# A graph aggregation by sorting: buckets in two parts of 36 and 23 a row instead of three of 29, 20 and 10

## The chip, the cores and the metric

The kernel runs on one core of one Trainium2 chip. The metric is the device time of one execution in microseconds, the median of several runs. In the profile PE is TensorE (PEld its weight loads), DVE is VectorE, ACT is ScalarE, POOL is GpSimd and SP is the engine that only issues transfers.

## The reference

12,500 nodes with 64 features each and 800,000 edges, drawn at random. For every node the features of the sources of its edges are summed, scaled and multiplied by a small matrix:

```python
N, deg, D = 12500, 64, 64          # E = N * deg edges
nsum = _segment_sum(x[src], dst, N)
h_neigh = nsum * deg_inv[:, None]
return x @ w_self + h_neigh @ w_neigh
```

## The kernel before, in words

The sum over edges is made of matrix products of one-hot matrices. For that the edges are sorted into 7,546 **buckets** (a bucket is one block of 128 source nodes with one block of destination nodes; about 106 edges fall in it). Bucket number `b` is one column of a table `sl` in DRAM and of a table `dlT` in SBUF. The work runs in these stages:

1. **Sort.** `make_keys` packs each edge into one 32-bit key, 6,250 keys in each of the 128 partitions. `sort_runs` (line 229, tiles `a` and `b`) sorts every partition with min and max instructions on VectorE. Its last 30 stages are cut along the row into portions, so that the front of the row is finished first. Each portion is a list of steps, and `after_sort` issues them by hand.
2. **Rows.** The buckets, rounded up to 7,552, are cut into parts, and a part into 128 rows of `KPRS[part]` buckets each. For every row `find_rows` counts on ScalarE where it starts in each of the 128 sorted runs (line 459, an activation with a sum), `gather_runs` then fetches with one indirect DMA of GpSimd for each row (line 474, tile `u`) a piece of `LENS[part][0]` keys of each run, and a small memset of `pad` behind it (`pause`). The sorted runs reach DRAM (`d1`) first, by transfers on SP. So before a row of part 0 is fetched, the sort must have finished up to column `CUT[0]`.
3. **Merge.** `merge_runs` merges the 128 pieces of every row on VectorE in 7 levels: first groups of pieces (`GROUPS`), then the groups. `merge_round` (line 285 the first two instructions of a round, line 297 the rest) does six levels; part 0's last level is `merge_last` (lines 316 and 331), whose lower half (up to `LOWER`) ends first.
4. **Buckets.** Each row is now sorted. `count_below` finds the boundary of each bucket in it (part 0 on ScalarE, line 636; the others on VectorE, line 633), an indirect DMA on GpSimd fetches a window for each (line 655, tile `v`), and `decode_buckets` turns the windows into `sl` and `dlT`. Keys that fell outside a window are the leftovers: a few VectorE instructions pick them (line 782), and later each group of rows fetches them with an indirect DMA (line 916, tile `lx`), and a matmul (line 933) adds them.
5. **The loop** (`nodes`): 950 tiles of 8 buckets. For each 28 buckets (3.5 tiles) SP loads `slb`, VectorE makes two one-hot matrices (line 854 `ohs`, line 859 `ohd`), TensorE gathers source features with `ohs` (line 885, into `ct`), ScalarE copies `ct` to `xg` (line 895; some copies go to VectorE, line 893, once `self.changed` is set), and TensorE sums with `ohd` (line 965, into `acc`).

The loop starts when part 0 is decoded. The other parts are merged and decoded inside it: between tiles `sums_and_merge` issues merge instructions on VectorE, as many nanoseconds of them for each tile as `PACE` says (450 for part 1, 335 for part 2). When all parts are decoded, `self.changed` becomes true and some of the copies move from ScalarE to VectorE.

Every engine executes its instructions in the order of issue; that order is the program's, and no scheduler changes it from the sort's last stages on.

Of the kernel before, what the change touches and what calls it, by code (L numbers as in the profile page):

```python
# [32 lines left out]
KPRS = (29, 20, 10)  # L33
# [3 lines left out]
TURN = -(-BASE[2] // 28) * 28  # L37
SPARE = TURN - BASE[2]
assert 128 * KPRS[2] < BASE[1]
# [6 lines left out]
PONG2 = 64 * LENS[2][0]  # L46
FIRST = 96
FROM_TILE = 50
BEFORE = 19
PACE = (0, 450, 335)  # L50
# [5 lines left out]
PCS = (19, 13, 9)  # L56
PCSN = 14
PIECES = (12, 4)
GRP = (2, 4, 7)
# [9 lines left out]
LOWER = 1770  # L69
CLOSE = 32  # L70
BEHIND = 6
NEARLY = 24
# [270 lines left out]
class Kernel:  # L343
# [136 lines left out]
    def merge_runs(self, part, u, pong):  # L480
# [25 lines left out]
        for n in GROUPS[part]:  # L506
            at = first * lens[0]
            level, rs, nr = 0, lens[0], n
            while nr > 1 + (part == 2):
                yield from round_(level, at, 0 if part == 2 else at, rs, nr, filler)  # L510
                rs, nr, level = 2 * lens[level], nr // 2, level + 1
# [4 lines left out]
            while part < 2 and len(done) > 1 and done[-1][0] == done[-2][0]:  # L516
# [8 lines left out]
        if part == 2:  # L525
            assert par[5] == 0 and par[6] == 1 and GROUPS[2] == (64, 64)
            for i in range(2):
                yield from round_(5, 64 * i * lens[0], 2 * i * lens[5], 2 * lens[4], 2)
            yield from round_(6, 0, 0, 2 * lens[5], 2)
# [160 lines left out]
    def decode_buckets(self, part, v, vp, mps):  # L690
# [31 lines left out]
        def turn(k, n, vk, l16):  # L722
# [4 lines left out]
            if part < 2:  # L727
                nc.scalar.activation(view(self.dlT, BASE[part] + k, [[kpr, 128], [1, n]]), ps, AF.Copy)
            else:
# [3 lines left out]
                for r in range(first):  # L733
                    edge = min(max(SPARE - r * kpr, k), k + n)
                    for a, e, to in ((k, edge, BASE[2]), (edge, k + n, -SPARE)):
# [389 lines left out]
    def after_sort(self, es, mps, aps):  # L1125
        tc = self.tc
        runs, run0, other = ExitStack(), ExitStack(), ExitStack()
# [5 lines left out]
        with tc.manual_schedule():  # L1133
            first, *portions, last = self.portions
# [4 lines left out]
            for i, step in enumerate(portions[0]):  # L1139
# [4 lines left out]
            u1, u0, pong = [stack.enter_context(tc.tile_pool(name=f"l2{i}", bufs=1))  # L1144
                            .tile([128, 128 * LENS[p][0] + more], F32, name="u")
                            for i, (stack, p, more) in enumerate(((runs, 1, 0), (run0, 0, 0), (other, 0, JUNK // 2)))]
            self.junk = pong[:, 128 * LENS[0][0]:].bitcast(BF)
            for i, step in enumerate(portions[1]):
# [16 lines left out]
            self.l1ab.close()  # L1165
            part = 1
            counts = None
            n = 0
            for _ in self.merge_runs(0, u0, pong):
                if rows and not self.hold and next(rows, None) is None:  # L1170
                    if part == 1:
                        gathers = self.gather_runs(1, u1)
                        for _ in range(FIRST):
                            next(gathers)
                        rows = self.find_rows(2, mps)
                        part = 2
                    else:
# [4 lines left out]
                        u2 = dl.tile([128, 128 * LENS[2][0]], F32, name="u2")  # L1182
# [8 lines left out]
            self.sums_and_merge(es, mps, aps, u0, u1, u2, runs, run0, other, counts, gathers)  # L1191
# [9 lines left out]
    def sums_and_merge(self, es, mps, aps, u0, u1, u2, runs, run0, other, counts, gathers):  # L1201
# [42 lines left out]
        for n in self.nodes(fin, aps, mps):  # L1244
# [10 lines left out]
            if chain is None and part + 1 < merging:  # L1255
                part += 1
                assert self.rows[part] is (u1, u2)[part - 1]
                if part == 2:
                    second.close()
# [70 lines left out]
```

## Time and profile before

| | |
|---|---|
| median of three runs | 1993.28 us (1989.81 to 2000.18) |
| profiled execution, its own time | 1997.82 us |
| its span in the profile | 1996.1 us |
| VectorE / ScalarE / TensorE / GpSimd busy | 1860.7 / 1316.4 / 963.1 / 1039.2 us |
| first fetch of a row of part 0 (line 474) | 422.9 us |
| first merge instruction (line 285) | 485.0 us |
| first one-hot (line 854), where the loop starts | 877.8 us |
| last one-hot | 1972.5 us |

A time such as 485.0 us counts from the start of the span. Rows of the timeline give the start, the duration, the engine, the line, what is written and read, and in square brackets the engine's idle time before it and what ended that time.

### The profile page before, as it was taken

To read this page: it belongs to the slowest core of one execution; us is meant where nothing else is said; L and a number is where in the kernel's file an instruction comes from. 1 tells how busy PE (TensorE), PEld (TensorE's weight loads), DVE (VectorE), ACT (ScalarE), POOL (GpSimd) and SP (SyncE) were. 2 spreads that over 40 slices of the span, in tenths; PEclk is the share of its full clock that TensorE was granted. 3 is DMA by queue.
4 is the path that set the end of the run, shared out by engine and by line. 5 is a ranking of instruction groups with operands and counts; after the bars stand their busy time and mean duration, and the time that the engine had idled before them with its cause. 6 is when DMAs were issued, how large, how long until landed. Compare 5 with 4: busy or idle time off the path is not lost.

```text
span 1996.1 us, 55979 instructions
## 1 busy us (share of the span) xinstructions
PE 963.1 (48%) x23311; PEld 853.6 (43%) x23311; DVE 1860.7 (93%) x2319; ACT 1316.4 (66%) x2288; POOL 1039.2 (52%) x1093
## 2 busy tenths in 40 slices
PE   0051000000000000025788888787698999879986
PEld 0041000000000000024677777776587888768875
DVE  8999999998999999998799999999899999988985
ACT  7371006538875004435799888888799999978885
POOL 1000000048888886799898997986232233432331
PEclk9965555555555555568899999988999999999998
DMA  4362000001100001257687888888588888978994
GB/s 147 65 147 46 0 0 18 17 26 39 19 19 18 14 15 44 62 170 186 183 243 235 249 236 246 238 280 247 162 245 260 267 257 255 304 206 265 276 263 111
DMA packets 193619, 303.51 MB, mean 152 GB/s; under 512 B 140921, under 2 KB 152483, under 8 KB 193100
## 3 DMA queue, kind: packets, MB, share of 16 engines
q1 hardware_dynamic: 98124, 273.66, 42.3%
q0 software_dynamic: 86656, 25.95, 9.3%
q8 instruction: 184, 3.01, 0.6%
q10 hardware_dynamic: 8576, 0.24, 0.3%
q14 instruction: 79, 0.65, 0.1%
HBM read 276.66 MB, written 22.65 MB: 150 GB/s over the span
## 4 chain that ended last, share of the span: by engine, by line
DVE 48%; POOL 13%; DMA 13%; issue 8%; PE 7%; ACT 5%; SPq 5%; DVEq 0%; POOLq 0%; ACTq 0%
DMA slb<-sl 12%; DVE u L297 11%; DVE b L229 9%; POOL u L474 8%; DVE a L229 8%; DVE ohs L854 7%; DVE ohd L859 6%; SPq L852 5%; PE ct L885 4%; POOL v L655 3%; PE acc L965 3%; POOL pad L389 2%; ACT xg L895 2%; DVE u L285 2%; DVE u L331 2%
## 5 line engine op out<-in xcount | busy, mean ns | idle before, releaser
L895 ACT ACTIVATE xg<-ct 128x1024 f16<-128x1024 f32 x918 | 862.1, 1068 | 125.6 <-PE ct L885 116.8
L474 POOL DMA_INDIRECT u<-d,ix x384 | 531.7, 1385 | 442.3 <-DVE ix L466 374.0
L885 PE MATMUL ct<-xh,ohs 128*128 128x128 f16 x7546 | 538.2, 225 | 64.0 <-DVE ohs L854 26.1
L297 DVE TENSOR_TENSOR u<-u 128x560 f32<-128x560 f32 (+44 forms) x738 | 498.7, 704 | 27.1 <-ACT u L281 17.6
L885 PEld LDWEIGHTS <-ohs 128*128 128x128 f16 x7546 | 458.9, 101 | 96.3 <-issue 44.8
L965 PE MATMUL acc<-ohd,xg 64*128 64x82 f16 x15092 | 399.2, 202 | 60.2 <-ACT xg L895 39.3
L965 PEld LDWEIGHTS <-xg 64*128 64x128 f16 x15092 | 328.6, 97 | 118.8 <-ACT xg L895 43.2
L859 DVE TENSOR_TENSOR ohd<-iota,dlT 128x2296 f16<-128x2296 bf16 x270 | 362.5, 1342 | 0.2 <-PE acc L965 0.2
L916 POOL DMA_INDIRECT lx<-xt,ls x127 | 202.6, 1595 | 297.6 <-PE acc L933 266.2
L854 DVE TENSOR_SCALAR ohs<-slb,pidx 128x3584 f16<-128x3584 bf16 x270 | 326.5, 1209 | 28.0 <-PE ct L885 16.0
L464 PE MATMUL stp<-idf,st 128*128 128x128 f32 x3 | 1.4, 466 | 480.5 <-DVE st L462 480.5
L229 DVE TENSOR_TENSOR b<-a 128x820 f32<-128x820 f32 (+52 forms) x184 | 214.8, 1215 | 7.0 <-ACT a L231 3.1
L459 ACT ACTIVATE junka<-b,c 128x220 bf16<-128x220 f32 (+46 forms) x384 | 170.5, 444 | 70.5 <-DVE b L229 59.4
L464 PEld LDWEIGHTS stp<-idf,st 128*128 128x128 f32 x3 | 0.5, 182 | 481.3 <-issue 263.2
L229 DVE TENSOR_TENSOR a<-b 128x820 f32<-128x820 f32 (+49 forms) x170 | 198.5, 1211 | 4.7 <-ACT b L231 2.3
L281 ACT ACTIVATE u<-u 128x167 f32<-128x167 f32 (+13 forms) x143 | 55.4, 452 | 176.4 <-DVE u L285 171.2
L1041 POOL DMA_DIRECT2D out<-o x27 | 99.0, 3798 | 58.6 <-ACT o L1035 58.4
L725 PE MATMUL tr<-idb,l 128*128 128x128 bf16 x59 | 8.0, 275 | 224.3 <-ACT l L719 224.3
L231 ACT ACTIVATE a<-b 128x1 f32<-128x1 f32 (+44 forms) x57 | 23.2, 422 | 136.1 <-DVE b L229 133.4
L389 POOL MEMSET pad<- 128x100 f32 x445 | 106.0, 238 | 2.0
L655 POOL DMA_INDIRECT v<-d,ix x59 | 79.0, 1339 | 47.3 <-DVE ix L666 21.6
L725 PEld LDWEIGHTS <-l 128*128 128x128 bf16 x59 | 4.6, 119 | 226.8 <-ACT l L719 226.4
(141 smaller groups left out, 838.7 us busy)
## 6 DMA issues: line engine op xcount, KB each, us to landing
slb<-sl SPq DMA_DIRECT2D x1076, 224.0 KB
u<-d,ix POOLq DMA_INDIRECT x384
xt<-xh SPq DMA_DIRECT2D x1, 3136.0 KB
out<-o POOLq DMA_DIRECT2D x25, 123.0 KB
own<-os SPq DMA_DIRECT2D x12, 256.0 KB
out<-os SPq DMA_DIRECT2D x12, 256.0 KB
rd<-dst SPq DMA_DIRECT2D x4, 521.0 KB
rs<-src SPq DMA_DIRECT2D x4, 521.0 KB
```

The lines of the kernel that those rows point to most:

```text
L229: nc.vector.tensor_tensor(view(dst, lo + sh, [[st, g], [1, l]]), x, y, op=op)
L297: nc.vector.tensor_tensor(to, at(cur, ln + lo, n), at(cur, lo + k, n), op=op)
L389: self.nc.gpsimd.memset(self.pad, 0.0)
L459: nc.scalar.activation(junk[:, :n], w, AF.Sign, bias=self.c1[:, 0, c:c + 1], accum_out=a)
L474: nc.gpsimd.indirect_dma_start(out=u[:nr, p * w:(p + 1) * w], out_offset=None, in_=src, in_offset=bass.IndirectOffsetOnAxis(ap=self.start[ ...
L655: self.nc.gpsimd.indirect_dma_start(out=self.v[:, k].bitcast(F32), out_offset=None, in_=flat(self.d2[part], 128 * PITCH2[part]), in_offset ...
L854: nc.vector.tensor_scalar(s.rearrange("p c s -> p (c s)"), b, self.pidx[:, :1], None, op0=OP.is_equal)
L859: nc.vector.tensor_tensor(d, self.iota[:, None].to_broadcast(wide), ix, op=OP.is_equal)
L885: nc.tensor.matmul(ct[:, i * 128:(i + 1) * 128], cols[i][0], self.xh[:, (b0 + i) % NB].rearrange("p a f -> p (a f)"), start=True, stop=True)
L895: nc.scalar.activation(xg[:, :cnt * 128], ct[:, :cnt * 128], AF.Copy)
L916: nc.gpsimd.indirect_dma_start(out=x, out_offset=None, in_=self.xt, in_offset=bass.IndirectOffsetOnAxis(ap=self.left[p][1][:, c:c + 1].bit ...
L965: nc.tensor.matmul(acc[h][:, db % OCT * HN:(db % OCT + 1) * HN], xg[r, i * 128:(i + 1) * 128], d[r], start=db % OCT == 0 and sb == 0, stop ...
```

## The change

The three parts of 29, 20 and 10 buckets a row become two parts of 36 and 23. The sort's last stages come in three portions instead of four. Part 2 disappears with its 128 row fetches, its merges, its bucket search and its decoding; part 0 and part 1 grow. `PACE` is one number, 400, and `u1` takes the place in memory that the sort leaves, as `u2` did.

The core of the diff (smaller cases for `part == 2` are left out of `merge_runs`, `decode_buckets` and `sums_and_merge`):

```diff
-KPRS = (29, 20, 10)
+KPRS = (36, 23)
-LENS = ((56, 92, 156, 280, 504, 936, 1776, 3424),
-        (44, 72, 120, 208, 368, 676, 1264, 2412),
-        (32, 48, 72, 124, 204, 368, 676, 1264))
-GROUPS = ((32, 32, 32, 32), (64, 32, 32), (64, 64))
+LENS = ((68, 112, 188, 336, 612, 1140, 2176, 4204),
+        (48, 80, 132, 228, 408, 760, 1440, 2752))
+GROUPS = ((32, 32, 32, 32), (64, 32, 32))
+COUNTS = 1
-PACE = (0, 450, 335)
+PACE = 400
-PCS = (19, 13, 9)
-PCSN = 14
+PCS = (23, 15)
+PCSN = 19
-GRP = (2, 4, 7)
+GRP = (2, 3)
-LOWER = 1770
+LOWER = 2200
-NEARLY = 24
+NEARLY = 32
@@ after_sort
-            first, *portions, last = self.portions
+            first, portion, last = self.portions
...
-            for i, step in enumerate(portions[1]):
+            for i, step in enumerate(last):
                 step()
                 while i < BEFORE and next(rows) + 1 < EARLY + (128 - EARLY) * (i + 1) // BEFORE:
                     pass
...
                     for _ in self.gather_runs(0, u0):
                         pass
-            tc.nc.sync.dma_start(self.d1[1], self.runs[:, FROM[1]:CUT[1]])
+            tc.nc.sync.dma_start(self.d1[1], self.runs[:, FROM[1]:])
+            self.l1ab.close()
             rows = self.find_rows(1, mps)
-            for step in last:
-                step()
-                for _ in range(2):
-                    next(rows)
-            tc.nc.sync.dma_start(self.d1[2], self.runs[:, FROM[2]:])
...
             for _ in self.merge_runs(0, u0, pong):
-                if rows and not self.hold and next(rows, None) is None:
-                    if part == 1:
...
+                for _ in range(COUNTS):
+                    if rows and not self.hold and next(rows, None) is None:
...
@@ sums_and_merge
-            if gathers and n % 2 and self.picked < n - 1:
-                if next(gathers, None) is None:
-                    gathers = None
-                else:
-                    gathered.append(n)
-            t += PACE[min(merging, 2)]
+            t += PACE
```

**What SP writes of the sorted runs.** The widths are columns of the sorted row; the first two are part 0, up to `CUT[0]` (3,362 columns before, 4,112 now). Before:

```order
L1137 DMA d_0_60<-b 128x1722
L1143 DMA d_0_60<-b 128x1640
L1158 DMA d_1_61<-b 128x2558
L1164 DMA d_2_62<-b 128x1316
L643 DMA d_0_71<-u 128x1770
L646 DMA d_0_71<-u 128x1654
```

Now:

```order
L1131 DMA d_0_60<-b 128x2104
L1137 DMA d_0_60<-b 128x2008
L1152 DMA d_1_61<-b 128x2760
L637 DMA d_0_68<-u 128x2200
L640 DMA d_0_68<-u 128x2004
```

The third write of before is gone, and part 0's reaches 750 columns further. (The last two rows of each are part 0's merged rows.)

**VectorE, where the sort ends and the merges of part 0 begin.** Before, the end of the narrow last portion (403 columns for each of the two instructions of a stage):

```order
L229 TENSOR_TENSOR b<-a 128x1
L229 TENSOR_TENSOR a<-b 128x133x3 x2
L229 TENSOR_TENSOR b<-a 128x200x2 x2
L229 TENSOR_TENSOR a<-b 128x201x2 x2
L229 TENSOR_TENSOR b<-a 128x403 x2
L229 TENSOR_TENSOR a<-b 128x403 x2
L229 TENSOR_TENSOR b<-a 128x404 x2
L285 TENSOR_TENSOR u<-u 128x16x56 x2
L297 TENSOR_TENSOR u<-u 128x16x24 x2
```

Now, the end of the portion in which the row fetches are issued (1,068 columns):

```order
L228 TENSOR_TENSOR b<-a 128x1
L228 TENSOR_TENSOR a<-b 128x355x3 x2
L228 TENSOR_TENSOR b<-a 128x533x2 x2
L228 TENSOR_TENSOR a<-b 128x534x2 x2
L228 TENSOR_TENSOR b<-a 128x1068 x2
L228 TENSOR_TENSOR a<-b 128x1068 x2
L228 TENSOR_TENSOR b<-a 128x1069 x2
L284 TENSOR_TENSOR u<-u 128x16x68 x2
L296 TENSOR_TENSOR u<-u 128x16x36 x2
```

The portion of 30 stages that stood between the fetches of part 0 and its first merge is gone; the first merge now follows the ten stages that are left of the portion in which the fetches are issued.

**VectorE in the loop, at about the 170th pair of one-hots (tile 595).** Before:

```order
L854 TENSOR_SCALAR ohs<-slb,pidx 128x3584
L859 TENSOR_TENSOR ohd<-iota,dlT 128x2296
L297 TENSOR_TENSOR u<-u_2124 128x2x189
L925 TENSOR_SCALAR ohl<-wide,lp_17466 128x2x82
L297 TENSOR_TENSOR u<-u_2124 128x2x182
L297 TENSOR_TENSOR u_2124<-u 128x2x186
```

Now:

```order
L919 TENSOR_SCALAR ohl<-wide,lp_19115 128x2x82
L887 CAST xg<-ct 128x1024
L848 TENSOR_SCALAR ohs<-slb,pidx 128x3584
L853 TENSOR_TENSOR ohd<-iota,dlT 128x2296
L968 COPY g<-acc_19038 128x6x82
```

The merges of part 2 between the one-hots are gone, and copies of `ct` stand there, which ScalarE made before.

More of the change, by code (lines that the diff above doesn't have):

```diff
@@ L508, in merge_runs @@
             level, rs, nr = 0, lens[0], n
[L509 to L510 removed]
+            while nr > 1:
+                yield from round_(level, at, at, rs, nr, filler)
                 rs, nr, level = 2 * lens[level], nr // 2, level + 1
@@ L1254, in sums_and_merge @@
                         lefts[p][1] = n + wait
[L1255 to L1259, printed above, removed]
-                vp = work.enter_context(tc.tile_pool(name=f"v{part}", bufs=1))
-                chain = self.change(part, vp, mps)
+            if part == 0 and not merge:
+                part = 1
+                assert self.rows[1] is u1
+                vp = work.enter_context(tc.tile_pool(name="v1", bufs=1))
+                chain = self.change(1, vp, mps)
                 last = None
```

82 lines of the change are left out of this document (29 added, 53 removed).

## The prediction

> **What bounds the kernel now.** I read the page's shares of busy time first:
>
> ```profile
> PE 963.1 (48%) x23311; PEld 853.6 (43%) x23311; DVE 1860.7 (93%) x2319; ACT 1316.4 (66%) x2288; POOL 1039.2 (52%) x1093
> ```
>
> VectorE is busy nearly everywhere, but 93% is a mean, so I cut the span at the events of the program and asked for the busy time in each stretch. The columns are the stretch, its length, busy time (and instructions) of PE, PEld, DVE, ACT and POOL, the granted clock, the share of the DMA engines, and GB/s:
>
> ```profile
> 422.80:481.00 58.20, 0.00 (x0) 0.00 (x0) 53.09 (x102) 33.19 (x134) 51.48 (x94) 0.50 0.13 38
> 481.00:485.00 4.00, 0.00 (x0) 0.00 (x0) 0.01 (x1) 1.72 (x6) 3.46 (x8) 0.50 0.56 188
> 485.00:790.00 305.00, 0.95 (x2) 0.36 (x2) 289.15 (x398) 132.80 (x483) 269.60 (x380) 0.50 0.09 19
> 790.00:806.70 16.70, 0.00 (x0) 0.00 (x0) 13.92 (x28) 15.03 (x32) 0.00 (x0) 0.50 0.12 51
> 806.70:877.80 71.10, 4.55 (x29) 2.52 (x29) 67.90 (x119) 24.45 (x48) 64.49 (x83) 0.50 0.27 74
> 877.80:982.90 105.10, 64.33 (x1520) 56.90 (x1520) 84.34 (x134) 61.99 (x71) 95.18 (x91) 0.82 0.71 202
> 982.90:1350.10 367.20, 313.55 (x7778) 278.24 (x7774) 364.81 (x477) 321.37 (x415) 323.85 (x283) 0.95 0.84 247
> 1350.10:1527.90 177.80, 141.45 (x3408) 124.55 (x3410) 166.71 (x254) 150.40 (x201) 69.90 (x47) 0.92 0.76 224
> 1527.90:1972.60 444.70, 395.77 (x10236) 355.14 (x10238) 407.56 (x512) 391.08 (x494) 147.41 (x78) 0.97 0.86 258
> 1797.20:1972.60 175.40, 159.80 (x4279) 145.28 (x4279) 152.10 (x148) 145.43 (x168) 48.45 (x24) 0.98 0.87 257
> 1972.60:1996.00 23.40, 7.29 (x204) 6.36 (x196) 5.53 (x8) 4.53 (x11) 5.34 (x3) 0.75 0.16 13
> ```
>
> Three regimes are to be seen. From the first row fetch (422.8) to the loop (877.8) VectorE sorts, merges and decodes, and almost nothing else counts. In the loop from 982.9 to 1350.1 it is busy 364.8 of 367.2 us: one-hots and merges share it, so each merge instruction delays the tiles. After 1797 there are no merges; VectorE idles 23 of 175 us while TensorE is busy 91% of the time and the DMA engines 87%: the tiles have a floor of their own there, 175.4 us for 49 pairs of one-hots, **3.58 us a pair** of 3.5 tiles.
>
> So a microsecond of VectorE before the loop costs a microsecond; one taken out of the loop is worth a microsecond only down to that floor.
>
> **Prices.** Two lengths of the same instruction give VectorE's slope:
>
> ```profile
> 421.87 2.39 DVE L229 TENSOR_TENSOR a<-b 128x1040 f32<-128x1040 f32 x2
> 476.15 1.07 DVE L229 TENSOR_TENSOR a<-b 128x402 f32<-128x402 f32 x2 [0.26 <-ACT b L231]
> 484.99 2.13 DVE L285 TENSOR_TENSOR u<-u 128x896 f32<-128x896 f32 x2 [4.05 <-POOL pad L389]
> ```
>
> (2.39 - 1.07) / 2 / 638 elements is 1.034 ns an element, and 2.39 / 2 less 1,040 of these leaves 0.12 us an instruction.
>
> The Trainium skill (Vector Engine (DVE) Microarchitecture Reference, 5.2 Measured stream behaviour on trn2) states 1.04 ns a column and about 75 ns an instruction after overlap. The slope agrees; the fixed part here is 0.12 us, and I take the row. With the page's 75 ns the loop's credit below, for 204 instructions, would be 9 us smaller, and the sum 2047 us.
>
> **a. The sort before the fetches.** Part 0 now needs 4,112 sorted columns instead of 3,362 (the writes of `d1` on SP, above). Each of the last 30 stages handles each column once, in a min or a max: 750 x 30 x 1.034 ns = **23.3 us** later. The first fetch moves from 422.9 to 446.2, and no cover exists: VectorE is the only worker here.
>
> **b. The cover of the fetches.** The first merge needs 32 fetches of GpSimd:
>
> ```profile
> 422.89 1.13 POOL L474 DMA_INDIRECT u<-d,ix  x1 [373.98 <-DVE ix L466]
> 434.26 1.83 POOL L474 DMA_INDIRECT u<-d,ix  x1 [0.16 <-issue]
> 480.84 0.95 POOL L474 DMA_INDIRECT u<-d,ix  x1 [0.15 <-issue]
> ...
> 629.07 1.21 POOL L474 DMA_INDIRECT u<-d,ix  x1 [0.16 <-issue]
> ```
>
> From the first (422.89) past the 32nd (480.84) to the merge (484.99) takes 62.1 us. Before, 58 us of sorting covered it, and VectorE waited 4.05 us. Now only ten stages of 2 x 1,068 elements are left, 10 x 2 x 1.22 = 24.5 us: the sort ends at about 470, the fetches at 446.2 + 62.1 = 508.3, and **VectorE waits 38 us instead of 4**. In time this adds nothing to a, since both sides come to the same 508.3; what is lost is 36 us of useful work (the old third portion) that once lay in that wait. Nothing in VectorE's order can fill it. The fetches' own price is bounded: at 0.95 us each (beside an idle VectorE) with the gaps and the two memsets 1.7 us, 32 make 54 us, 4 fewer than the 58 here; at 1.83 us, as beside long sort instructions, 2.43 us or 78 us. Before, about ten ran at the slow price and the rest faster; now again ten meet long instructions and the rest an idle engine, so I keep 62.1, range 58 to 82.
>
> The Trainium skill says (SBUF — State Buffer, Who interferes with whom) that a VectorE instruction with two SBUF inputs contends with a GpSimd instruction that reads SBUF; 1.83 us against 0.95 us agrees with it. Were all 32 fetches held back so, the first merge would come 20 us later; but VectorE is idle for most of them.
>
> **c. Part 0's merges.** By `merge_plan` and `LENS`, part 0 grows from 233,018 elements in 376 instructions to 290,260 in 388: 57,242 x 1.034 ns + 12 x 0.12 = **60.6 us**, all on the path (VectorE is busy 289 of 305 us there). GpSimd's 128 + 96 row fetches run beside them as before: part 1's start when part 0's are issued (629.07, quoted above, 206 us after the first), now at about 446 + 206 = 652 us, in time for its merges after 870.
>
> **d. Search, windows, decoding.**
>
> ```profile
> 804.62 0.85 ACT L636 ACTIVATE u<-u,c 128x667 bf16<-128x667 f32 x1
> 806.72 0.95 POOL L655 DMA_INDIRECT v<-d,ix  x1 [21.64 <-DVE ix L666]
> 855.07 1.44 POOL L655 DMA_INDIRECT v<-d,ix  x1 [0.16 <-issue]
> ```
>
> ScalarE's counts behind the last merge are 15 in 14.7 us now; 18 of up to 738 elements make 18.7, **4 us** more. The 29 window fetches take 48.35 / 28 = 1.73 us each; 7 more are **12.1 us**. VectorE is as full as GpSimd here, with 6 us of extra merges of part 1 and 3 of decoding, which fit inside.
>
> The loop starts at 877.8 + 23.3 + 60.6 + 4 + 12.1 = **977.8**, 100 us later.
>
> **e. The loop.** What VectorE no longer does in it, by counting its instructions behind the first one-hot: merges fall from 426 instructions and 207,216 elements to 222 and 127,194, 204 x 0.12 + 80,022 x 1.034 ns = 107 us. Bucket counts rise from 13,607 elements in 30 (line 633, 20.4 us) to 28,376 in 23, some 34 us, so 14 more. Copies rise from 32 to 67:
>
> ```profile
> L895 ACT ACTIVATE xg<-ct 128x1024 f16<-128x1024 f32 x918 | 862.1, 1068 | 125.6 <-PE ct L885 116.8
> L893 DVE CAST xg<-ct 128x1024 f16<-128x1024 f32 x32 | 39.0, 1220 | 24.4 <-PE ct L885 23.7 <-issue 0.5 <-ACT o L1035 0.3
> L297 DVE TENSOR_TENSOR u<-u 128x560 f32<-128x560 f32 (+44 forms) x738 | 498.7, 704 | 27.1 <-ACT u L281 17.6
> L633 DVE TENSOR_SCALAR_CACHE_REDUCE junk<-u,c 128x103 bf16<-128x103 f32 (+29 forms) x30 | 20.4, 680 | 0.1
> ```
>
> 35 x 1.22 = 43 us, given away by ScalarE, only where VectorE has room. By stretch, cut at the same pairs of one-hots as above:
>
> - 20 pairs from 877.8: before 105.1 us with 20.8 of idle. One wait is most of it:
>
> ```profile
> 956.84 1.24 DVE L854 TENSOR_SCALAR ohs<-slb,pidx 128x3584 f16<-128x3584 bf16 x1 [12.91 <-PE ct L885]
> 951.62 0.95 POOL L916 DMA_INDIRECT lx<-xt,ls  x1 [0.16 <-issue]
> ```
>
>   TensorE waited for the first leftovers (`lx`), which stood behind 14 row fetches of part 2 in GpSimd's queue. Those are gone; `lx` follows part 1's last fetch directly. 105.1 - 12.9 - 3 of fewer merges = 89.2.
> - 90 pairs (982.9 to 1350.1): 315 tiles. `PACE` falls from 450 to 400 ns for about 275 of them (13.8 us) and rises from 335 for 40 (2.6); part 1's search (some 9 us of line 633) moves out. 367.2 - 20 = 347.2, above the floor of 90 x 3.58 = 322.
> - 40 pairs (1350.1 to 1527.9): part 2's merges leave (40 us), part 1's rest, search and decoding come (12 of merges, 34 of counts): 177.8 - 3 = 175, against a floor of 143.
> - 119 pairs (1527.9 to 1972.6): no merge and no part is left, so the floor: 119 x 3.58 = 426 instead of 444.7. VectorE's removed work is worth 19 us here, not the 49 of its merges.
>
> Sum 1037.4 instead of 1094.8, **57 us back**. With 23.4 behind the last one-hot as before the span is 977.8 + 1037.4 + 23.4 = **2038.6** against 1996.1, 2.1% more. The profiled execution took 1997.82, 1.7 above its span and 0.23% above the median of 1993.28; on that scale 2040.3 is **2036 us**.
>
> **The rivals.**
>
> *The loop gives all of it back* (same or faster). Its floor could be lower than 3.58: in that stretch TensorE is busy 159.8 of 175.4 us. If the tiles ran at that, the last 119 pairs take 388 us, and with the third stretch at VectorE's bare sum (165) the span is 1990.6, -0.3%. It decides once the loop is under 995 us. For it speaks that GpSimd has little left to do; against it that ScalarE and VectorE, relieved, did not reach it in the 49 pairs seen. Chance 0.13.
>
> *VectorE's total decides* (faster). The sort and the merges lose 246 instructions and 13,396 elements, 43 us; at 93% busy the span would follow, to 1953. Against it: 34 us of new idle before the merges, and the floor. The Trainium skill's rule (VectorE: DVE Perf Modes, Rules for kernel authors) to minimize the operation count speaks for this case; the trace bears it out only where VectorE is full. Chance 0.05.
>
> *Part 1's search stalls the tiles* (slower still). Its windows now reach 2,278 elements, 2.4 us in a piece before a one-hot, 23 times; if TensorE loses 1.1 us at each, 25 us more: 2064 in the span, about 2061. Before, the two chains cost 11.1 us of VectorE idle in 1350 to 1528. Chance 0.17.
>
> My own sum has 0.65, with 2010 to 2060. To leave out no more than 2 in 10, the range is 2000 to 2062: most of the first rival is outside it. 0.5% is about what a measurement here can tell: slower by more 0.82, within 0.08, faster 0.10.
>
> **What would show it.** Right: first fetch near 446, a VectorE wait of some 35 us ended by GpSimd before the first merge, part 0's merges about 365 us long, first one-hot near 978, no 13 us wait for `lx`, and about 3.6 us a pair from tile 525 on. Wrong: a first one-hot before 950, or fewer than 3.4 us a pair in the last stretch.

## The result, and the profile after

The changed kernel takes **2057.42 us** (median of four runs, 2051.18 to 2061.83) against 1991.68 for the kernel before in the same comparison: ratio 1.0319, 95% interval 1.0278 to 1.0361 (times are medians, ratios here and below are of means). The forecast was 2036 with 2000 to 2062: the sign and the range held, the size was 21 us short. The profiled execution took 2055.87 us, its span is 2054.1. Its busy times, to set beside the line of before:

```profile
PE 954.5 (46%) x23292; PEld 852.0 (41%) x23292; DVE 1866.9 (91%) x2040; ACT 1223.4 (60%) x1965; POOL 808.0 (39%) x825
```

VectorE does the same amount of work, 1866.9 us against 1860.7, in 58 us more. So nearly all of the loss is idle time of VectorE, and three windows show where it lies: up to the first row fetch, from there to the first one-hot, and the loop. First before, then after (columns as in the prediction: length, then busy time of PE, PEld, DVE, ACT and POOL):

```profile
0.00:422.80 422.80, 35.26 (x152) 29.53 (x152) 407.63 (x300) 179.80 (x398) 8.48 (x32) 0.64 0.20 52
422.80:877.80 455.00, 5.50 (x31) 2.88 (x31) 424.07 (x643) 207.19 (x703) 389.03 (x563) 0.50 0.13 33
877.80:1972.60 1094.80, 915.09 (x22934) 814.83 (x22936) 1023.42 (x1372) 924.85 (x1177) 636.34 (x496) 0.94 0.82 243
```

```profile
0.00:446.10 446.10, 37.93 (x152) 31.88 (x152) 429.79 (x318) 180.84 (x411) 7.30 (x29) 1.00 0.20 50
446.10:992.40 546.30, 5.93 (x37) 3.29 (x37) 473.54 (x595) 159.09 (x456) 411.58 (x581) 1.00 0.13 31
992.40:2031.40 1039.00, 902.46 (x22883) 809.70 (x22884) 957.69 (x1123) 877.84 (x1088) 383.80 (x213) 0.95 0.84 252
```

Length less the third busy time is VectorE's idle time: 15.2, 30.9 and 71.4 us before, 16.3, 72.8 and 81.3 after. The work moved from the loop (65.7 us less there) to the front (71.6 us more), as the change says; on the way 42 us of idle time appeared in the middle window and 10 in the loop.

The stages of the changed kernel in the cut of the prediction (part 0's merges, counts behind them, windows and decoding, then 20, 90, 40 and 119 pairs of one-hots, and the tail):

```profile
505.80:885.50 379.70, 0.48 (x1) 0.18 (x1) 352.81 (x409) 111.36 (x355) 280.43 (x382) 1.00 0.09 18
885.50:905.90 20.40, 0.00 (x0) 0.00 (x0) 18.29 (x30) 18.63 (x38) 0.04 (x1) 1.00 0.12 50
905.90:992.40 86.50, 5.45 (x36) 3.10 (x36) 78.69 (x136) 27.60 (x56) 78.47 (x101) 1.00 0.28 77
992.40:1075.50 83.10, 67.26 (x1566) 60.15 (x1566) 81.43 (x123) 61.67 (x68) 55.13 (x47) 0.90 0.84 248
1075.50:1419.80 344.30, 304.24 (x7743) 271.14 (x7738) 340.98 (x410) 315.32 (x398) 113.30 (x49) 0.98 0.84 250
1419.80:1606.50 186.70, 145.06 (x3408) 127.21 (x3405) 166.86 (x233) 150.09 (x215) 81.35 (x55) 0.90 0.77 234
1606.50:2031.40 424.90, 385.90 (x10177) 351.20 (x10177) 368.42 (x362) 350.75 (x410) 134.02 (x62) 0.97 0.87 263
2031.40:2054.00 22.60, 8.17 (x224) 7.16 (x221) 5.84 (x8) 5.67 (x11) 5.33 (x3) 0.77 0.16 14
```

And the two rows at the seam between sort and merges, the first fetch and the first merge instruction, with the idle time of each engine before it:

```profile
446.15 1.15 POOL L473 DMA_INDIRECT u<-d,ix  x1 [397.33 <-DVE ix L465]
505.81 1.29 DVE L284 TENSOR_TENSOR u<-u 128x1088 f32<-128x1088 f32 x1 [35.49 <-POOL pad L388]
```

| step | forecast, us | measured, us |
|---|---|---|
| first fetch | 446.2 | 446.15 |
| first merge (VectorE's wait before it) | 508.3 (38) | 505.8 (35.5) |
| part 0's merges | 365.6 | **379.7** |
| counts behind them | 20.7 | 20.4 |
| windows and decoding | 83.2 | 86.5 |
| first one-hot | 977.8 | 992.4 |
| loop by 20 / 90 / 40 / 119 pairs | 89.2 / 347.2 / 175 / 426 | 83.1 / 344.3 / 186.7 / 424.9 |
| loop | 1037.4 | 1039.0 |
| tail | 23.4 | 22.7 |

One term is off by much: part 0's merges, by 14 us of the 15.5 that the span missed. The rest of the 21 us is how far a profiled execution lies from the median: the one of before, on which the sum was scaled, was 4.5 us over its median of then, and this one is 1.6 under.

Where the 14 us are, the groups of instructions of that stretch tell (busy time, mean of one, idle time before them and what ended it). After, VectorE's two lines and ScalarE's copies; then the same of before, in its stretch of 305.0 us:

```profile
L296 DVE TENSOR_TENSOR u<-u 128x752 f32<-128x752 f32 (+29 forms) x324 | 263.3, 845 | 24.5 <-ACT u L280 18.0
L280 ACT ACTIVATE u<-u 128x512 f32<-128x512 f32 (+12 forms) x62 | 29.9, 520 | 253.1 <-DVE u L284 252.5
```

```profile
L297 DVE TENSOR_TENSOR u<-u 128x704 f32<-128x704 f32 (+28 forms) x312 | 214.5, 728 | 12.5 <-ACT u L281 7.5
L281 ACT ACTIVATE u<-u 128x512 f32<-128x512 f32 (+10 forms) x62 | 23.0, 432 | 126.0 <-DVE u L285 126.0
```

VectorE's busy time grew by 63.7 us (289.15 to 352.81), 3 more than forecast. Its idle time grew by 11 (15.9 to 26.9), and the forecast had no growth there: 10.5 of that are waits for ScalarE's copies in `merge_round` (line 280: keys that a round leaves where they are still have to be copied to the other buffer).

A round shows how. After its first two instructions (line 284) ScalarE copies, and VectorE goes on with the pair of the first distance. VectorE in one group of 32 pieces, rounds of 8, 4 and 2 pairs of runs, and ScalarE's copies in the last of these:

```profile
524.02 0.58 DVE L296 TENSOR_TENSOR u<-u 128x168 f32<-128x168 f32 x2 [0.88 <-ACT u L280]
524.96 11.08 DVE L296 TENSOR_TENSOR u<-u 128x640 f32<-128x640 f32 x12 [0.36 <-ACT u L280]
539.07 11.43 DVE L296 TENSOR_TENSOR u<-u 128x388 f32<-128x388 f32 x14 [1.20 <-ACT u L280]
550.53 1.63 DVE L284 TENSOR_TENSOR u<-u 128x672 f32<-128x672 f32 x2
553.88 3.36 DVE L296 TENSOR_TENSOR u<-u 128x82 f32<-128x82 f32 x6 [1.72 <-ACT u L280]
```

```profile
552.19 1.66 ACT L280 ACTIVATE u<-u 128x590 f32<-128x590 f32 x3 [4.35 <-DVE u L284]
```

The last round is the clearest: line 284 ends at 552.16, the three copies run from 552.19 to 553.85, and VectorE's first pair starts at 553.88. It doesn't run beside the copies; it waits for them to their end. The program's order with the semaphores that each instruction waits for says the same. These are the first pairs of those rounds, now and, in the round of 4 pairs of runs, before:

```
352 L296 TENSOR_TENSOR u<-u 128x8x21 [waits Activation_49]
368 L296 TENSOR_TENSOR u<-u 128x4x97 [waits DVE_49,Activation_49]
384 L296 TENSOR_TENSOR u<-u 128x2x41 [waits DVE_49,Activation_49]
...
427 L297 TENSOR_TENSOR u<-u 128x4x65 [waits DVE_49]
```

`Activation_49` is ScalarE's semaphore. In part 0's 22 rounds in `merge_round` the first pair carries this wait 12 times now and 4 before; VectorE's idle time ahead of these first pairs adds up to 15.6 us now and 3.1 before. Where it doesn't, at most a later pair waits, and the first covers the copies for as long as it lasts. The same round of before:

```profile
509.55 1.53 DVE L285 TENSOR_TENSOR u<-u 128x624 f32<-128x624 f32 x2
511.11 0.77 DVE L297 TENSOR_TENSOR u<-u 128x260 f32<-128x260 f32 x2
512.14 8.65 DVE L297 TENSOR_TENSOR u<-u 128x496 f32<-128x496 f32 x12 [0.26 <-ACT u L281]
```

The round ahead of it has a first pair of 8 elements (0.26 us for both instructions), and its second pair waits 1.38 us.

The new sizes did two things at once: they made copies longer (590 elements for each pair of runs in the last round shown, where the plan's first distance was 64 and is 128, instead of 182), and they put the wait ahead of the first pair in eight more rounds. By the plan, the ranges that pair and copies write do not overlap; why the wait is set in some rounds and not in others was not found. No run moves the wait alone, so how the 10.5 us divide between the two is not shown. The kernel has a switch, `late`, that issues the copies behind the first instruction of the first pair; it is off in part 0, and no run turned it on there.

### The profile page after: what moved, and what is told of

The parts are those of the page before. It is cut to its first block, busy times and chain, and to the rows that moved or that the text cites. A ratio compares the mean times of both kernels' runs of the same rounds, so it can differ in the third digit from the quotient of the medians.

```text
span 2054.1 us, 55077 instructions
## 1 busy us (share of the span) xinstructions
PE 954.5 (46%) x23292; PEld 852.0 (41%) x23292; DVE 1866.9 (91%) x2040; ACT 1223.4 (60%) x1965; POOL 808.0 (39%) x825
## 4 chain that ended last, share of the span: by engine, by line
DVE 22%; DMA 13%; PE 12%; issue 7%; POOL 6%; ACT 5%; SPq 3%; DVEq 0%; ACTq 0%; POOLq 0%
DMA slb<-sl 11%; DVE u L296 7%; PE ct L879 6%; DVE ohs L848 5%; PE acc L959 4%; DVE ohd L853 4%; ACT xg L889 3%; POOL u L473 3%; SPq L846 3%; POOL v L649 2%; DVE u L330 2%; DVE u L284 1%; POOL pad L388 1%; ACT u L630 1%; DMA lk<-lt 1%
## 5 line engine op out<-in xcount | busy, mean ns | idle before, releaser
L889 ACT ACTIVATE xg<-ct 128x1024 f16<-128x1024 f32 x883 | 831.4, 1057 | 132.2 <-PE ct L879 109.2
L473 POOL DMA_INDIRECT u<-d,ix x256 | 332.1, 1297 | 440.5 <-DVE ix L465 397.3
L296 DVE TENSOR_TENSOR u<-u 128x570 f32<-128x570 f32 (+43 forms) x578 | 464.4, 831 | 33.0 <-ACT u L280 23.9
L959 PE MATMUL acc<-ohd,xg 64*128 64x82 f16 x15092 | 389.3, 202 | 52.2 <-ACT xg L889 22.6
L910 POOL DMA_INDIRECT lx<-xt,ls x118 | 211.4, 1792 | 510.3 <-PE acc L927 495.8
L228 DVE TENSOR_TENSOR b<-a 128x1008 f32<-128x1008 f32 (+44 forms) x154 | 211.3, 1421 | 4.2 <-ACT a L230 0.3
L280 ACT ACTIVATE u<-u 128x512 f32<-128x512 f32 (+14 forms) x110 | 50.0, 507 | 272.0 <-DVE u L284 271.5
L228 DVE TENSOR_TENSOR a<-b 128x1008 f32<-128x1008 f32 (+38 forms) x140 | 194.8, 1436 | 4.0 <-ACT b L230 2.0
L458 ACT ACTIVATE junka<-b,c 128x220 bf16<-128x220 f32 (+44 forms) x256 | 115.3, 450 | 47.1 <-DVE b L228 39.8
L230 ACT ACTIVATE a<-b 128x1 f32<-128x1 f32 (+44 forms) x57 | 23.4, 425 | 165.6 <-DVE b L228 162.8
L887 DVE CAST xg<-ct 128x1024 f16<-128x1024 f32 (+1 forms) x67 | 80.9, 1209 | 45.2 <-PE ct L879 35.9
```

The source lines that it names most:

```text
L228: nc.vector.tensor_tensor(view(dst, lo + sh, [[st, g], [1, l]]), x, y, op=op)
L296: nc.vector.tensor_tensor(to, at(cur, ln + lo, n), at(cur, lo + k, n), op=op)
L458: nc.scalar.activation(junk[:, :n], w, AF.Sign, bias=self.c1[:, 0, c:c + 1], accum_out=a)
L473: nc.gpsimd.indirect_dma_start(out=u[:nr, p * w:(p + 1) * w], out_offset=None, in_=src, in_offset=bass.IndirectOffsetOnAxis(ap=self.start[ ...
L889: nc.scalar.activation(xg[:, :cnt * 128], ct[:, :cnt * 128], AF.Copy)
L910: nc.gpsimd.indirect_dma_start(out=x, out_offset=None, in_=self.xt, in_offset=bass.IndirectOffsetOnAxis(ap=self.left[p][1][:, c:c + 1].bit ...
```

## The experiments

Experiments 1 to 4, 5 to 8 and 9 to 11 ran in three groups, each beside runs of the kernel before. Spans and events are of profiled executions; up to the first one-hot those of the same kernel repeat within 1.5 us, the loop's last stretch within 5.

**1. The sort in four portions again.** The cut at column 5,442 comes back, and the last columns are sorted while the fetches run.

```diff
-    for last in [SPLIT] + CUT[:-1]:
+    for last in [SPLIT] + CUT[:-1] + [5442]:
...
-            first, portion, last = self.portions
+            first, portion, last, tail = self.portions
...
+            for step in tail:
+                step()
```

> The changed kernel with the sort's last stages cut in four portions again: the portion in which the row fetches of part 0 are issued ends at column 5442 (1330 columns instead of 2138), and the last 958 columns are sorted behind the fetches, as before the change. Mine (the lost cover costs nothing by itself, the later fetch does): the 20 stages ahead of the first fetch are 17 us shorter for VectorE, but ScalarE needs some 40 us there for 64 row counts of 0.63 us, so the first fetch comes about 8 us earlier (438 instead of 446), the first merge at about 498, VectorE's wait before it shrinks from 35 to about 20 us, and the time falls by about 8 us, to some 2049 against the changed kernel's 2057. Rival (the lost cover itself costs the 31 us by which the wait grew): about 2026.

Measured: 2033.16 us, ratio to before 1.0167 (1.0125 to 1.021). The first fetch comes at 438.8, and the wait shrinks from 35.5 us to 7.6:

```profile
492.94 1.29 DVE L284 TENSOR_TENSOR u<-u 128x1088 f32<-128x1088 f32 x1 [7.60 <-POOL pad L388]
```

The first one-hot comes 12.8 us earlier (979.6). So filling 28 of the 35.5 us of idle time was not worth 28: it moves VectorE's work from before the fetches to beside them, and the merges still can't start before 32 fetches are done. The chain gains 7.3 us by the earlier first fetch and 5.3 because the fetches themselves take 51.4 us instead of 56.7 up to the 32nd. The loop took 1028.5, 10 us less than in the profile above and 6 less than in the control below, nearly all of it in the last stretch (416.3), for which no mechanism was found. In time the gain was 24 us, between my 8 and the rival's 31; the part of it ahead of the loop has the cause above.

**2. Smaller first groups**: two groups of 16 in place of the first 32, so that the merges wait for 16 fetches.

```diff
-GROUPS = ((32, 32, 32, 32), (64, 32, 32))
+GROUPS = ((16, 16, 32, 32, 32), (64, 32, 32))
```

> The changed kernel with part 0's first group of 32 runs cut in two groups of 16, so that the first merge needs 16 fetches instead of 32. Mine (VectorE stands still there for want of fetches, and each microsecond of it is on the path): the first merge at about 483 instead of 506, some 28 us of merging run while the other 16 rows are fetched; against it stand about 46 more merge instructions (5 us) and more waits for ScalarE's copies (3 us). About 15 us less than the changed kernel: 2042. Rival (only VectorE's sum of work counts): 5 us more, 2062.

Measured: 2051.40 us, 1.0252 (1.0201 to 1.0302).

```profile
481.14 1.48 DVE L284 TENSOR_TENSOR u<-u 128x544 f32<-128x544 f32 x2 [10.80 <-POOL pad L388]
```

The first merge comes 24.7 us earlier, the first one-hot only 10.5 (981.9): the extra group has rounds and instructions of its own (64 more instructions, where 46 were expected, and 25.5 us of waits for copies instead of 18.0), and their price takes back more than half.

**3. Shorter distances** in the plan of the rounds, to give the copies and the first pairs other sizes.

```diff
-SIGMA = 6.0
+SIGMA = 5.5
```

> The changed kernel with a bound of 5.5 sigma instead of 6 on how far a key can stand from its place when two runs are merged. With it part 0's fourth and sixth merge levels need no distance of 128 and 256, as in the kernel before, where the shorter runs did not need them, and ScalarE's copies of the untouched keys between two merge instructions are shorter (26182 to 22028 elements over part 0). Mine (the 14 us by which part 0's merges came out longer than forecast are this: VectorE's waits for ScalarE's copies, 18.0 instead of 7.5 us, and the extra steps): about 5 us of instructions and 9 us of waits less before the loop, 2043. Rival (the excess is VectorE slowed by GpSimd's fetches, or waits for the fetches): the 5 us of instructions alone, 2052.

Measured: 2048.40 us, 1.0249 (1.0203 to 1.0294). Part 0's merges take 373.8 us instead of 379.7, and the first one-hot comes at 985.9.

```profile
L296 DVE TENSOR_TENSOR u<-u 128x864 f32<-128x864 f32 (+29 forms) x312 | 259.3, 862 | 22.5 <-ACT u L280 16.3
```

The first distances are those of the kernel before again, but the waits only fell from 18.0 to 16.3 us; the other 4.4 are instructions. So the length of the distance, my first reading of the 14 us, is not what makes VectorE wait. That led to the rows on the semaphores above: in this kernel, too, the first pair carries the wait in three of the five rounds of a group.

**4. Fewer merges for each tile.**

```diff
-PACE = 400
+PACE = 350
```

> The changed kernel with 350 instead of 400 ns of merge instructions a tile in the loop, so that part 1's merges end some 50 tiles later. Mine (the loop has a floor of about 3.58 us a pair of one-hots, and VectorE's work counts only where a pair exceeds it): pairs with merges fall from 3.83 to about 3.66 us, and fewer pairs are left at the floor: about 14 us less, 2043. Rival (VectorE's sum decides the loop, so where its work stands makes no difference): 2057.

Measured: 2040.99 us, 1.0203 (1.0149 to 1.0258). The loop's stretches:

```profile
992.30:1072.30 80.00, 64.12 (x1519) 57.06 (x1520) 78.31 (x119) 60.30 (x67) 64.08 (x46) 0.91 0.90 254
1072.30:1403.30 331.00, 301.63 (x7727) 268.75 (x7726) 328.97 (x399) 311.46 (x393) 117.03 (x49) 0.98 0.88 260
1403.30:1565.50 162.20, 137.97 (x3424) 122.69 (x3424) 157.78 (x161) 141.26 (x183) 72.20 (x43) 0.93 0.84 256
1565.50:2017.00 451.50, 397.90 (x10257) 358.14 (x10252) 387.23 (x438) 372.58 (x459) 142.16 (x76) 0.96 0.85 252
```

1024.7 instead of 1039.0. The merges move 27 us into the last stretch, where VectorE had room, and the three stretches ahead of it, where VectorE is the limit, give 41 back. This is the split that the forecast of the loop was made by.

**5. The changed kernel once more**, as a control for the next three.

> The changed kernel once more, unchanged, beside the next three kernels on one chip, so that each of them can be compared with it event by event. Expected: first one-hot within 2 us of 992, span 2050 to 2060. If the loop's last 119 pairs differ by more than 5 us from the 425 of the first profile, differences of that size in the last stretch of other kernels mean nothing.

Measured: 2055.67 us, 1.0294 (1.0247 to 1.034); first one-hot 991.8, span 2049.1, the stretches 83.1, 344.4, 186.2 and 420.8. Up to the last stretch all repeats within half a microsecond; the last is 4 us shorter.

**6. Part 0's size alone**: three parts and four portions as before, but part 0 at 36 buckets a row.

```diff
-KPRS = (29, 20, 10)
+KPRS = (36, 13, 10)
-LENS = ((56, 92, 156, 280, 504, 936, 1776, 3424),
-        (44, 72, 120, 208, 368, 676, 1264, 2412),
+LENS = ((68, 112, 188, 336, 612, 1140, 2176, 4204),
+        (36, 60, 92, 156, 264, 472, 868, 1640),
```

> The kernel before with its first part at the new size and the rest still in two: 36, 13 and 10 buckets a row, four portions of the sort, three parts. Theory (the size of part 0 costs, wherever the rest is cut): first fetch at 446, part 0's merges about 380 us, first one-hot between 975 and 1000, 100 to 120 us later than before; in the loop the merges of parts 1 and 2 shrink by 50 us of VectorE only, so the loop takes about 1055 and the span about 2065. Rival (the two parts and the three portions cost, not part 0's size): the first one-hot stays near 900 and the span under 2010.

Measured: 2065.82 us, 1.0337 (1.0291 to 1.0383); first one-hot 979.1, span 2063.3; the loop's stretches 88.6, 387.6, 144.8 and 440.3. Part 0's merges and what lies between them and the loop:

```profile
492.40:872.90 380.50, 0.95 (x2) 0.37 (x2) 353.26 (x410) 142.63 (x491) 283.08 (x382) 0.50 0.08 17
872.90:979.10 106.20, 5.48 (x36) 3.11 (x36) 91.10 (x189) 46.43 (x97) 76.66 (x115) 0.50 0.25 71
```

Part 0's merges take 380.5 us, as in the changed kernel (379.7). The size of part 0 alone costs 101 us ahead of the loop, of which the loop gives 33 back. Cutting the rest into one part instead of two, and the sort into three portions instead of four, is then worth 9 us to the good (2063.3 to 2054.1): 13.3 lost before the loop, 22.3 won in it.

**7. ScalarE's copies twice**, in part 0's merges; the second writes the same values again.

```diff
     def both():
-        for a, e in alone:
-            nc.scalar.activation(at(src, a, e - a), at(oth, a, e - a), AF.Copy)
+        for _ in range(2 if ln in LENS[0] else 1):
+            for a, e in alone:
+                nc.scalar.activation(at(src, a, e - a), at(oth, a, e - a), AF.Copy)
```

> The changed kernel, with each of ScalarE's copies of untouched keys in the merges of part 0 issued twice (the second rewrites the same values). Those 62 copies take 29.9 us of ScalarE. Theory (VectorE stands still for these copies at nearly every level: its first pair of a level waits for their end where an order row shows an Activation wait on it): part 0's merges get 18 to 30 us longer, 398 to 410 instead of 380, and the first one-hot comes at 1010 to 1022. Rival (the copies are hidden behind VectorE's own pairs, and the idle time seen is a fixed signal delay): under 5 us longer.

Measured: 2075.95 us, 1.0379 (1.0336 to 1.0422); first one-hot 1015.7, 23.8 us later than the control. VectorE's line and the copies in that stretch:

```profile
L297 DVE TENSOR_TENSOR u<-u 128x752 f32<-128x752 f32 (+29 forms) x324 | 263.0, 844 | 47.7 <-ACT u L281 41.7
L281 ACT ACTIVATE u<-u 128x512 f32<-128x512 f32 (+12 forms) x124 | 58.8, 519 | 247.1 <-DVE u L285 245.7
```

28.9 us more of copies make 23.7 us more of VectorE's waits, at the same busy time. So VectorE pays four fifths of each microsecond that these copies take: the rival, a fixed delay of signals, is out.

**8. Groups of 32, 32 and 64**: 82 instructions and five rounds fewer for the same elements.

```diff
-GROUPS = ((32, 32, 32, 32), (64, 32, 32))
+GROUPS = ((32, 32, 64), (64, 32, 32))
```

> The changed kernel with part 0's 128 pieces merged in groups of 32, 32 and 64 instead of four of 32: the same 290,260 elements in 82 instructions fewer and five rounds fewer. Theory (each instruction costs 0.12 us beside its elements, and each round has its own wait for ScalarE's copies): part 0's merges 9.8 us shorter by the instructions and 2 to 5 by the waits, so 365 to 368 instead of 380, first one-hot at 977 to 981. Rival (the group of 64 waits for its last row fetch): the fetches end near 655 and the group starts near 650, so a wait of about 5 us there, and 3 to 7 us of gain in all.

Measured: 2050.38 us, 1.027 (1.0221 to 1.0318); first one-hot 989.6, only 2.2 us earlier than the control. The group of 64 found its last pieces missing, for longer than the 5 us that the rival gave it:

```profile
662.00 2.43 DVE L284 TENSOR_TENSOR u<-u 128x2176 f32<-128x2176 f32 x1 [12.48 <-DMA u<-d,ix]
L296 DVE TENSOR_TENSOR u<-u 128x768 f32<-128x768 f32 (+40 forms) x252 | 254.8, 1041 | 20.1 <-ACT u L280 14.8
```

Beside that wait the parts came as priced. Line 296 is busy 254.8 us instead of 263.3, and line 284 42.6 instead of 43.8 (34 and 44 instructions): 9.7 us for 82 instructions, 0.118 each. The waits for copies fell by 3.2. The Trainium skill (Vector Engine (DVE) Microarchitecture Reference, 5.2) gives about 75 ns an instruction; an estimate by it would be 6.2 us. The 9.7 us measured decide for the prediction's 0.12.

**9. No copies of `ct` on VectorE**: ScalarE makes all of them.

```diff
-            pend.append(gather(b0, cnt, self.changed))
+            pend.append(gather(b0, cnt, False))
```

> The changed kernel without the 67 copies of `ct` that VectorE takes over once all parts are decoded: ScalarE makes all 950. Theory (the last 119 pairs run at a floor that TensorE and the DMA engines set, and the copies only fill VectorE's room): the stretch stays at 421 to 430 us and the span within 6 us of 2052. Rival (ScalarE is just as near its limit, and the floor of 3.5 us a pair exists only because VectorE takes these copies): 67 copies of 0.94 us make ScalarE up to 63 us longer, of which it has some 40 free, so the stretch takes 440 to 455.

Measured: 2056.72 us; ratio 1.0176 (1.0107 to 1.0245), in a group of runs in which the kernel before itself took 2022.89, some 25 us more than in the others, so that this ratio and the next two aren't set beside earlier ones. First one-hot 992.8, and the last 119 pairs:

```profile
1608.00:2029.00 421.00, 386.96 (x10168) 347.54 (x10168) 313.93 (x315) 394.73 (x469) 119.61 (x63) 0.98 0.89 268
```

421.0 us, as in the control (420.8), with ScalarE busy 394.7 instead of 350.8 and VectorE 313.9 instead of 368.3. Neither sets the floor of the last stretch. What is left near its limit in that row is TensorE (387 of 421) and the DMA engines (0.89); which of the two it is, no run tells.

**10. What helped, together**: the four portions, the pace of 350, and one pause behind each of the first 32 fetches (`CLOSE = 0` instead of 32).

> What helped the changed kernel, together: the sort in four portions again, 350 ns of merges a tile instead of 400, and one pause instead of two behind each of the first 32 row fetches. Theory (the parts add up: they act at different places): first merge near 486 and first one-hot at 972 to 976, the loop 14 us shorter than that of the four portions alone (1028.5), so a span of 2008 to 2014, still slower than before. Rival (the last stretch takes the 14 us back): a span near 2025.

Measured: 2037.22 us (median of ten), 1.0064 (1.0031 to 1.0098) to before in that group; beside the 1992 to 1999 us of before in the other groups it would be about 1.02. The profiled execution took 2045.76 us, the longest of the ten, so some 8 us of the loop below are likely that execution's alone. First merge 491.2: the second pause was worth 1.7 us, not 7. The 32 fetches were issued in 47.4 us instead of 51.4, but the merge then started 4.2 us after the end of the last of them instead of 1.8. First one-hot 978.4, and the loop 1043.0, where 1014 were expected:

```profile
978.50:1066.80 88.30, 69.69 (x1531) 61.20 (x1532) 78.36 (x119) 61.61 (x68) 54.21 (x45) 0.88 0.80 233
1562.40:2021.50 459.10, 398.19 (x10228) 357.49 (x10229) 386.35 (x438) 371.73 (x458) 140.20 (x76) 0.96 0.83 248
```

The rival had the direction: the first stretch is 8 us longer and the last 8 us longer than with the pace alone, with the same busy time of VectorE and a DMA share of 0.80 and 0.83 instead of 0.90 and 0.85. In the first stretch most of it is not this kernel's doing. The kernel of experiment 9 has there the instructions of the changed kernel, which took 83.1 us for it in both profiles, and in this group of runs it took 89.0:

```profile
992.80:1081.80 89.00, 70.53 (x1566) 60.92 (x1566) 81.50 (x122) 62.13 (x68) 42.44 (x44) 0.86 0.79 232
```

What made that group slower there, and whether it also made the last stretch longer, stays open.

**11. Two parts of 33 and 26**, with four portions. Part 1 has to be ready sooner, which takes a pace of 500.

```diff
-KPRS = (36, 23)
+KPRS = (33, 26)
...
-PACE = 400
+PACE = 500
```

> The changed kernel with two parts of 33 and 26 a row instead of 36 and 23, four portions of the sort, and 500 ns of merges a tile (fewer and part 1 would not be ready when the tiles reach it). Theory (three buckets a row fewer in part 0 save about 42 us before the loop, and the loop pays about two thirds of it back as merges of part 1): first merge near 486, first one-hot at 934 to 942, the loop 1050 to 1062, the span 2008 to 2024. Rival (the loop pays nothing, since its floor is the tiles'): a loop of 1030 and a span of 1990. Third (VectorE's total decides, the span stays): 2028 to 2034.

Measured: 2042.89 us, 1.0108 (1.0041 to 1.0176) in the same group; first one-hot 929.8, loop 1086.8, span 2039.0.

```profile
929.80:1020.70 90.90, 70.20 (x1535) 61.03 (x1536) 87.10 (x127) 62.59 (x71) 59.93 (x49) 0.89 0.78 228
1020.70:1394.70 374.00, 314.32 (x7719) 279.57 (x7716) 370.07 (x428) 316.04 (x395) 124.27 (x54) 0.93 0.77 229
1394.70:1596.50 201.80, 149.04 (x3417) 129.20 (x3410) 175.29 (x241) 153.18 (x222) 82.27 (x60) 0.88 0.72 219
```

My forecast of the loop failed. 50 us saved before it (against the first experiment) came back as 58 in it, nearly all in the three stretches up to the 150th pair, and the span moved by 8. About 6 of the 58 are the first stretch's, which that group of runs made longer for experiment 9 too. That is nearest to the third case, that VectorE's total decides: its busy time is 12 us longer than in the first experiment (1886.2 and 1874.4). My reading is that two thirds would be paid back only if the merges that move into the loop found room there; here they all stand ahead of the 110th pair, where VectorE is nearly full (370 of 374 us in the second stretch), and none in the last stretch, where it is not.

**12. The kernel before, against itself.**

> The kernel before once more, unchanged, timed against itself and profiled, since it was 1993, 1999, 1999 and 2023 us beside the groups of runs so far while the changed kernel stayed near 2056. Expected: a ratio of 1 with an interval that holds 1 (0.995 to 1.005). The stages up to the first one-hot repeat within 2 us (first merge 485, first one-hot 878); theory: what differs from look to look lies in the loop's stretches (105.1, 367.2, 177.8, 444.7 in the first profile), above all in the last. Rival: it lies before the loop.

Measured: 1995.86 against 1996.7 us, ratio 0.9987 (0.9966 to 1.0008). First merge 485.0, first one-hot 879.1, the loop's stretches 104.4, 366.7, 175.2 and 442.0: the profile that the forecast was read from repeats within 3 us in each. The 2022.89 of the group above was not seen again and is not explained.

No version of the changed kernel was faster than the kernel before.

## Why the prediction was right, and where it was not

- **The sort before the fetches** (a) and **the cover of the fetches** (b) came as worked out: first fetch 446.15 for 446.2, wait 35.5 for 38, first merge 505.8 for 508.3. That the wait adds nothing to the later first fetch is shown by the first experiment: filling 28 us of it moved the first one-hot by 12.8, and that by the fetches. It also shows that "nothing in VectorE's order can fill it" was wrong: the end of the sort can, and with less of the sort ahead of them the fetches start 7.3 us earlier.
- **Part 0's merges** (c) is the step that was mis-sized: 60.6 us priced, 74.7 measured. Elements and instructions were within 3 us. The sentence "VectorE is busy 289 of 305 us there" was taken for "nothing waits", and the 16 us of idle time were left as they were, though 7.5 of them were waits for ScalarE's copies that grow with the part, and whose cover depends on which instruction carries the wait. Doubling the copies showed the price of that term (23.7 us for 28.9).
- **Search, windows, decoding** (d): counts 20.4 for 20.7; windows and decoding 86.5 for 83.2, since the 36 fetches took 1.80 us each up to the last (905.9 to 969.0 for 35 of them) instead of 1.73.
- **The loop** (e): 1039.0 and 1034.5 for 1037.4. The floor of the last stretch held: 3.57 and 3.54 us a pair for 3.58, and experiment 9 shows that ScalarE's and VectorE's shares are not behind it. The 13 us wait for the first `lx` is gone. The 40 pairs around part 1's search are 11.7 us longer than forecast, against 9 us won in the two stretches ahead, so that the total came this close partly by luck. Bucket counts there are busy 34.4 us, as forecast. Of the 11.7 us, 3 are busy time that the forecast took off and that did not go, and 8.7 are idle time of VectorE (19.8 us there, 11.1 before). The 3 came from terms that do not add up as written: 40 us that leave and 12 and 34 that come make 6 more, and only with line 285's 8.6 us of before 3 less. Nor is the idle time the third rival's (the search stalls the tiles): the counts run from 1440 to 1515, and VectorE's waits from 1534 to 1562, behind them, are 13.8 us, while part 1 is decoded. The longest is a chain. ScalarE waits 6.02 us for a transfer of the decoding (`sl<-l`) before it goes on to copy `ct`, TensorE waits 7.78 us for that copy, and VectorE 4.98 us for TensorE; in the control the same chain waits 3.76, 5.52 and 3.54 us. VectorE's waits ahead of its one-hots in the stretch, then the three of the chain:

```profile
L848 DVE TENSOR_SCALAR ohs<-slb,pidx 128x3584 f16<-128x3584 bf16 x40 | 49.7, 1243 | 13.9 <-PE ct L879 7.3 <-DMA slb<-sl 6.7
1538.51 0.72 ACT L708 ACTIVATE l<-w,edge 128x512 bf16<-128x512 int32 x1 [6.02 <-DMA sl<-l]
1541.47 0.73 PE L959 MATMUL acc<-ohd,xg 64*128 64x82 f16 x16 [7.78 <-ACT xg L889]
1546.22 1.15 DVE L848 TENSOR_SCALAR ohs<-slb,pidx 128x3584 f16<-128x3584 bf16 x1 [4.98 <-PE ct L879]
```

- **The rivals.** That the loop gives all back needed a loop under 995 us; none of eleven profiles of the changed kernel and its variants was under 1024. That VectorE's total decides was wrong for this change (busy time up 6 us, span up 58). Its 43 us counted sort and merges alone; with the copies (43 us) and bucket counts (14 us) that (e) adds to VectorE, the prediction's own prices give 14 us more, not 43 less. Still, the last but one experiment shows that between two ways of cutting in two it comes close.
- **The sum by 75 ns an instruction** (2047 us) takes the whole 9 us off the loop's credit, though (e) adds the loop up by stretches and cuts the last one at its floor; by (e)'s own working less than 9 us of it would reach the sum.

## What to carry to other kernels

When work moves from a stage where it shares an engine with others to one where it runs alone, compare the engine's idle time by stage, not its total: here VectorE's work was the same to 6 us, and 52 of the 58 us lost were new idle time. Price the short waits inside a stretch that looks full: read what ends them, and ask whether that work grows with the change and which instruction carries the wait. An idle gap in front of a chain of transfers is worth only what the chain gets shorter, not its length.

## What the runs showed of the hardware that I had not expected

GpSimd's row fetch takes longer the longer the VectorE instructions beside it are; that VectorE is busy costs it little by itself. The fetches beside sort instructions of 1.2 us, beside an idle VectorE, and (first experiment) beside sort instructions of 0.25 to 0.5 us, with a row of VectorE from the first and the third:

```profile
L473 POOL DMA_INDIRECT u<-d,ix x10 | 18.5, 1848 | 398.7 <-DVE ix L465 397.3 <-issue 1.4
L473 POOL DMA_INDIRECT u<-d,ix x22 | 20.9, 950 | 3.4 <-issue 3.4
455.29 2.45 DVE L228 TENSOR_TENSOR a<-b 128x1065 f32<-128x1065 f32 x2
```

```profile
L473 POOL DMA_INDIRECT u<-d,ix x17 | 18.2, 1073 | 2.6 <-issue 2.6
458.99 0.99 DVE L228 TENSOR_TENSOR a<-b 128x288 f32<-128x288 f32 x4
```

1.85, 0.95 and 1.07 us. The Trainium skill (SBUF — State Buffer, Who interferes with whom) says that a VectorE instruction with two SBUF inputs contends with a GpSimd instruction that reads SBUF; the 1.85 us against 0.95 agree with it. The 1.07 us add that short instructions cost the fetch little even without a gap between them.

The granted clock in the rows is 0.50 up to the loop in some executions and 1.00 in others, while TensorE is all but idle there. The mean over an execution of the changed kernel was 0.766 with a span of 2049.5 us and 0.974 with 2054.1 and 2057.2, and in the control 0.762 with 2061.2 and 0.978 with 2049.1, so it says nothing of the time here.
